# A new order for all engines, and new slots, in a fused Mamba-2 scan and SiLU feed-forward kernel

## The chip, the cores and the metric

The kernel runs on one core of one Trainium2 chip. The metric is the device time of one execution in microseconds (us). Before the change its median is 339.22 us over three runs (338.0 to 340.31).

The engines of the core are named as in the profile: PE is TensorE (matmuls), with PEld for its weight loads; DVE is VectorE, ACT is ScalarE, POOL is GpSimd, SP is SyncE, which here only issues transfers. Each engine takes its instructions in the order of the program, and waits where an operand or a buffer isn't ready; what stands behind a waiting instruction on the same engine waits with it.

## What is computed

A chunked Mamba-2 state-space scan over four batches, eight heads and 768 positions, and then a feed-forward block with SiLU on its output, reshaped to 3072 tokens of 256 features.

```python
# scan: x (4, 8, 768, 32), a (4, 8, 768), B and C (4, 8, 768, 16), chunks of 32
log_a = np.log(np.clip(a, 1e-06, 1.0))
for c in range(nc):
    cum = np.cumsum(la, axis=-1)
    L = np.exp(cum[:, :, :, None] - cum[:, :, None, :]) * causal
    M = np.einsum('bhin,bhjn->bhij', Cc, Bc) * L
    y_intra = np.einsum('bhij,bhjd->bhid', M, xc)
    y_inter = np.einsum('bhin,bhnd->bhid', Cc, state) * np.exp(cum)[:, :, :, None]
    y[:, :, sl] = y_intra + y_inter
    decay_from_j = np.exp(cum[:, :, -1:] - cum)
    Bx = np.einsum('bhjn,bhjd->bhjnd', Bc, xc) * decay_from_j[:, :, :, None, None]
    state = decay_full[:, :, None, None] * state + np.sum(Bx, axis=2)
# feed-forward: w_in (256, 2048), w_out (2048, 256)
h = x @ w_in
g = h * (1.0 / (1.0 + np.exp(-h)))
return g @ w_out
```

## The kernel before

**Units and pairs.** The scan is cut into 12 units of 256 positions (u = 0 to 11, three for a batch), each made of four chunks of 64. Two units make a pair (G or P = 0 to 5) of 512 tokens, and the feed-forward block works on pairs. Its hidden layer of 2048 is cut into eight blocks of 256 (j or i = 0 to 7).

**The order is written out.** Under a manual schedule, the string SCHEDULE lists 1283 tokens, and a loop at the end of the kernel calls one function for each. A token is a name and its arguments, so `a,1,0` calls f_a(1, 0). The sequence of the tokens is at once the sequence of the instructions of every engine and that of the transfers in each queue. Waits between engines are put in from the data: an operand that isn't written yet, or a buffer that still has readers.

**The slots.** Tiles come from four pools with numbered slots: s2k (49 of 2 KB a partition), r4k (12 of 4 KB), raw (7 of 4 KB) and hp (3 PSUM banks). SLOTS holds, for each pool, the slot of the first tile taken, of the second, and so on. A new tile in a slot waits until the last reader of the old one is done. Two more PSUM tiles, ga and gb, and a bank, o_ps, are fixed.

**The work of a unit**, with its tokens:
- loads on SP: Lx (x), Ln (B and C by position), Lt (B and C for a transpose on DVE), La (the decays, broadcast from a DRAM copy az), Lp (from a DRAM copy ac). For u = 0 and 1 the decays are made on the chip: ia, ip, A, AT, AU, as, ab, P01.
- E (DVE scan) makes the decay matrix, P (DVE scan) the prefix products, T (DVE transpose, L524) or tp with tq (PE transpose and ACT copy) the transposed B and C; ce, C and B scale C and B.
- g0 (PE, L584) makes C times B, D or gd (PE, L570) the chunk states, M (DVE) the masked matrix, b, S and SM the states from chunk to chunk, Y (PE, L634 and L643) the output.
- X0 (units 0 and 1) or y, xh and x (the others) bring the output into the feed-forward block's form. xh and x make three parts, h, l and d, of a pair's x, rounded to a format that PE multiplies in one pass.

**The feed-forward block.** Weights come as raw 512 KB blocks (lw,0 to lw,15: eight of w_in, eight of w_out). u, v (ACT), w (DVE) and W (POOL) turn each into fp32. For pair 0 the products are plain fp32: s (PE, L695), si (ACT, SiLU), n1 (PE, L759), Vn. For the pairs 1 to 5 each weight is split into three parts by H (ACT), lD and dD (DVE), and the products run in single passes: a has the h and l parts of the first matmul (eight matmuls, L798), ax rescales it in PSUM (ACT), d adds the d part (four matmuls), dg is SiLU (ACT), h (ACT), l and e (DVE, L650 and L835) split the result, q (three matmuls of 128 by 512, L780) is the second product, summed in the banks of hp and o_ps. Va, Vd, o and O scale, add, transpose and store. The last half pair goes out by Vt, ot, or and os: PE transposes, two copies, two stores.

**Warm-up.** z,1 and z,0,6 are matmuls on zeros that PE does at the start, in places where it would stand idle. ct is a SiLU on one element.

Of the kernel before, what the change touches and what calls it, by code (L numbers as in the profile page):

```python
# [28 lines left out]
si,1,3 W,4 s,0,4 si,0,4 si,1,0 Lx,2,1,0 La,2,0,0 La,2,1,0 E,2,0 W,5 s,0,5 si,0,5 W,8 n1,1,1 n1,1,0 La,3,0,0 w,11,0
w,11,1 w,9,1 s,1,4 lw,12 v,12 AD,1 Ln,2,1,0,0 tp,2 v,7 u,12 W,11 tq,2 H,1 Lt,3,1,1,0 u,10 n1,7,0 si,1,4 w,12,0 Lx,3,0,0  # L30
n1,6,1 ce,2,0 n1,0,0 E,2,1 w,7,2 lw,6 v,6 w,9,2 n1,7,1 co n1,6,0 Lp,2,0 P,2 C,2 Lt,3,1,3,0 Lx,2,0,0 B,2 gd,2 ce,2,1 g0,2
lw,13 w,14,1 La,3,1,0 W,9 b,2,0 w,10,0 S,2,0 n1,2,1 w,10,1 Lt,3,0,0,0 W,7 H,5 H,9 Lt,3,1,0,0 b,2,1 u,6 S,2,1 S,2,2
SM,2,1 SM,2,0 n1,3,1 W,10 H,10 s,0,7 si,0,7 M,2,0 n1,4,1 Lt,3,0,1,0 n1,0,1 Ln,3,0,0,0 lw,15 n1,5,0 w,6,0 H,4 w,6,2 H,2
# [10 lines left out]
Vn,1 dD,9 dD,12 h,1,2 a,1,4 Lt,5,0,0,0 Lt,5,1,0,0 n1,15,0 dg,1,1 h,1,1 Lt,5,1,3,0 T,5,1 n1,14,0 dD,3 Vn,0 lD,11 e,1,0
a,1,3 E,5,1 ax,1,4 q,1,0,1,0 q,1,0,0,0 ax,1,3 d,1,3 Ln,5,0,0,0 ce,5,0 dD,4 d,1,4 l,1,1 Lt,6,1,0,0 e,1,1 q,1,1,1,1
q,1,1,0,0 dD,6 dg,1,3 o,0,0,2 o,0,1,2 dg,1,4 Lt,5,0,2,0 q,1,0,0,1 T,5,0 ce,5,1 g0,5 Lt,6,1,3,0 E,5,0 l,1,2 B,5 h,1,3 P,5
C,5 M,5,1 q,1,0,1,1 gd,5 b,5,0 b,5,1 dD,11 q,1,1,1,0 a,1,5 e,1,2 q,1,2,0,1 h,1,4 q,1,1,0,1 H,7 ax,1,5 d,1,5 S,5,0 S,5,1
q,1,2,0,0 Lx,6,1,0 S,5,2 SM,5,0 Lt,6,1,2,0 Lt,6,1,1,0 T,6,1 ce,6,1 ce,6,0 q,1,2,1,0 Lp,6,0 Lx,6,0,0 Lt,6,0,3,0 l,1,4
# [838 lines left out]
```

## Time and profile before

| | us |
|---|---|
| median of three runs | 339.22 |
| the profiled execution's own time | 341.09 |
| its span, first to last instruction | 339.4 |
| PE busy in the span | 323.2 |
| first matmul of a token s (L695) starts | 20.31 |
| first matmul of a token a (L798) starts | 76.92 |

The prediction shows the lines of the page and of the trace. A row of a timeline gives start, length (for merged rows, from the first start to the last end), engine, line, operation, output and inputs, shapes and count; in brackets stands the time that the engine was idle just before, and what ended that. A row of a group gives busy time, mean ns of one instruction, idle time before the group's instructions and the largest releasers. "SPq" is SP's queue of transfer issues.

The page gives the granted clock of PE in 40 slices: it is full but for the second slice, at 0.7, and the last. The page's list of transfers gives 512 KB for each weight, 3.3 us from issue to landing for w_in and 7.1 for w_out as medians.

### The profile page before, as it was taken

What the parts mean: (1) busy time and instruction counts of PE and PEld (TensorE: products, weight loads), DVE (VectorE), ACT (ScalarE), POOL (GpSimd) and SP (SyncE); (2) the same over time, 40 slices, a digit from 0 to 9 for tenths busy, and PEclk for the clock granted to TensorE, in tenths of its full rate; (3) what the DMA queues carried; (4) which work ended last, traced back from release to release, by engine and by line L of the source; (5) the groups of instructions that cost most, each with busy time, mean ns of one, the idle gap of its engine ahead of it and who ended that gap; (6) DMA issues with size and microseconds to landing.
All of it is one profiled execution on the core that took longest, in us unless ns stands there. A gap on an engine that the chain in (4) does not pass through costs nothing.

```text
span 339.4 us, 7527 instructions
## 1 busy us (share of the span) xinstructions
PE 323.2 (95%) x3086; PEld 243.8 (72%) x3086; DVE 251.1 (74%) x346; ACT 201.9 (59%) x307; POOL 50.1 (15%) x64
## 2 busy tenths in 40 slices
...
GB/s 190 150 304 258 186 241 135 37 139 32 110 70 14 58 52 105 32 50 111 19 22 114 63 26 132 21 50 131 30 2 92 23 2 2 8 62 1 2 0 62
DMA packets 93522, 26.64 MB, mean 79 GB/s; under 512 B 79840, under 2 KB 86752, under 8 KB 93488
## 3 DMA queue, kind: packets, MB, share of 16 engines
...
q10 hardware_dynamic: 2352, 0.26, 0.6%
...
## 4 chain that ended last, share of the span: by engine, by line
PE 78%; DVE 8%; DMA 6%; ACT 3%; SPq 3%; issue 2%; POOL 0%; DVEq 0%
PE hp L780 28%; PE gb L798 16%; PE ga L798 16%; PE o_ps L780 5%; DMA raw<-in_moe_w_out_dram 3%; PE hp L759 2%; PE hp L695 2%; DVE ab L599 2%; PE ga L584 2%; PE ga L634 1%; DVE st L614 1%; PE ga L643 1%; DMA xt<-in_x_dram 1%; PE ga L570 1%; DVE ab L511 1%
## 5 line engine op out<-in xcount | busy, mean ns | idle before, releaser
L780 PE MATMUL hp<-r4k,s2k 128*128 128x512 f32 x400 | 110.4, 395 | 0.0
L780 PEld LDWEIGHTS hp<-r4k,s2k 128*128 128x128 f32 x400 | 73.8, 188 | 16.7 <-issue 0.7
L650 DVE SCALAR_TENSOR_TENSOR r4k<-r4k,r4k 128x1024 fp32r<-128x1024 f32 x40 | 48.8, 1221 | 32.6 <-ACT r4k L825 20.7
L798 PE MATMUL ga<-raw,s2k 128*128 128x512 f32 x240 | 63.1, 397 | 0.5 <-DVE raw L650 0.5
L798 PE MATMUL gb<-raw,s2k 128*128 128x512 f32 x240 | 62.5, 396 | 0.9 <-DVE ab L599 0.9
L798 PEld LDWEIGHTS ga<-raw,s2k 128*128 128x128 f32 x240 | 44.6, 188 | 12.3 <-DVE raw L650 1.0
L798 PEld LDWEIGHTS gb<-raw,s2k 128*128 128x128 f32 x240 | 44.3, 188 | 12.7 <-DVE ab L599 1.4
L835 DVE SCALAR_TENSOR_TENSOR r4k<-r4k,r4k 128x1024 fp32r<-128x1024 f32 x40 | 49.2, 1233 | 2.1 <-PE o_ps L780 0.2
L825 ACT ACTIVATE r4k<-r4k 128x1024 fp32r<-128x1024 f32 x40 | 42.1, 1058 | 1.1 <-DVE r4k L650 0.4
L695 PE MATMUL hp<-r4k,s2k 128*128 128x256 f32 x128 | 30.0, 384 | 1.3 <-ACT r4k L701 0.6
L809 ACT ACTIVATE ga<-ga 128x1024 f32<-128x1024 f32 x20 | 20.2, 1010 | 18.3 <-PE ga L798 18.3
L759 PE MATMUL hp<-r4k,s2k 128*128 128x512 f32 x64 | 30.7, 605 | 0.3 <-POOL s2k L318 0.3
L780 PE MATMUL o_ps<-r4k,s2k 128*128 128x512 f32 x80 | 30.7, 390 | 0.0
L809 ACT ACTIVATE gb<-gb 128x1024 f32<-128x1024 f32 x20 | 20.1, 1007 | 16.3 <-PE gb L798 16.3
L695 PEld LDWEIGHTS hp<-r4k,s2k 128*128 128x128 f32 x128 | 23.8, 190 | 8.3 <-issue 2.7
L519 POOL TENSOR_TENSOR BT<-bn,ab 128x256 f32<-128x256 f32 x10 | 9.0, 899 | 128.7 <-DVE ab L511 78.6
L318 POOL TENSOR_TENSOR s2k<-s2k,s2k 128x512 uint32<-128x512 uint32 (+1 forms) x19 | 24.4, 1298 | 21.0 <-DVE s2k L307 13.5
L819 ACT ACTIVATE r4k<-ga 128x1024 f32<-128x1024 f32 x20 | 20.5, 1025 | 9.0 <-PE ga L798 8.4
L819 ACT ACTIVATE r4k<-gb 128x1024 f32<-128x1024 f32 x20 | 20.5, 1025 | 7.8 <-PE gb L798 6.8
L511 DVE TENSOR_TENSOR_SCAN ab<-ab,diag 128x512 f32<-128x512 f32 x20 | 23.8, 1207 | 1.0 <-DMA ab<-az 1.0
L759 PEld LDWEIGHTS hp<-r4k,s2k 128*128 128x128 f32 x64 | 11.4, 189 | 9.9 <-issue 8.4
L780 PEld LDWEIGHTS o_ps<-r4k,s2k 128*128 128x128 f32 x80 | 15.0, 188 | 3.3
...
## 6 DMA issues: line engine op xcount, KB each, us to landing
...
```

What stands on the lines that cost most here:

```text
L318: nc.gpsimd.tensor_tensor(out=u[:, :, fs], in0=u[:, :, fs], in1=v[:, :, fs], op=ALU.add)
L511: nc.vector.tensor_tensor_scan(out=o, data0=src, data1=diag.rearrange("p h t -> p (h t)"), initial=0.0, op0=ALU.mult, op1=ALU.add)
L519: nc.gpsimd.tensor_tensor(out=BT[u][:, ks], in0=bn[u][:, ks], in1=E[u][:, ks, :, Q - 1:Q].to_broadcast([128, n, H, N]), op=ALU.mult)
L650: nc.vector.scalar_tensor_tensor(out=l, in0=f32(h), scalar=BACK, in1=y, op0=ALU.mult, op1=ALU.add)
L695: nc.tensor.matmul(out=hp[:, i], lhsT=WT[j][:, kc, 128 * i:128 * i + 128], rhs=XM()[:, 2 * kc:2 * kc + 2, u], start=(kc == 0), stop=(kc == ...
L759: nc.tensor.matmul(out=NP[m], lhsT=WT[8 + f // 2][:, f % 2, 128 * m:128 * m + 128], rhs=GT[0, f // 2][:, f % 2], start=(n == 1), stop=(n = ...
L780: nc.tensor.matmul(out=ACC[P, c], lhsT=WK[8 + i, p][:, k, 128 * m:128 * m + 128], rhs={"h": HT, "l": LT, "d": DT}[p][P, i][:, k], start=(n ...
L798: nc.tensor.matmul(out=o, lhsT=WK[j, q][:, kc, 128 * i:128 * i + 128], rhs=xs[:, 2 * kc:2 * kc + 2], start=(start and q == "h" and kc == 0 ...
L809: nc.scalar.activation(t, t, AF.Copy, scale=1.0 + Z)
L819: nc.scalar.activation(g, t, AF.Silu, scale=BACK)
L825: nc.scalar.activation(t, GT[G, i], AF.Copy, scale=-LESS * Z)
L835: nc.vector.scalar_tensor_tensor(out=DT[G, i], in0=f32(HT[G, i]), scalar=-1.0, in1=f32(LT[G, i]), op0=ALU.mult, op1=ALU.subtract)
```

## The change

The string SCHEDULE is replaced by another order of the same 1283 tokens, each with the same arguments and as often as before. SLOTS is replaced for all four pools, with as many entries as before. Two functions get a case for the pair 0. No operation, shape or transfer is changed.

The start of the two orders:

```diff
-ci z,1 z,1 z,1 z,0,6 z,0,6 ct z,1 z,1 cp lw,0 Ln,0,0,1,1 z,1 c1 cd z,1 ch cP ia,1 ia,0 v,0 w,0,2 cI ip,0,0 P01,0,0 u,0
...
-v,1 Ln,1,0,1,0 B,1,1 S,0,2 SM,0,1 M,0,1 ir,0 ab,1,0 E,1,0 SM,0,0 Ln,1,0,0,0 B,1,0 tp,1 ce,1,0 tq,1 ce,1,1 Y,0 w,1,0 ir,1
-ip,1,0 P01,1,0 X0,0,1 X0,0,0 S,0,3 Lx,1,1,0 w,1,1 w,1,2 W,1,0 W,1,1 P01,1,1 Lx,1,0,0 D,1 S,1,0 S,1,1 C,1 S,1,2 lw,3
-SM,1,1 w,2,0 w,2,1 W,2,0 lw,7 W,2,1 u,7 ca g0,1 M,1,1 lw,4 s,0,0 si,0,0 SM,1,0 v,3 AA,1 M,1,0 lw,9 Lx,3,1,0 u,3 AD,0 u,9
+lw,0 c1 ca ci cI z,1 z,1 co z,1 cp cd z,1 z,0,6 z,1 u,0 ia,0 ia,1 z,1 lw,2 z,0,6 ch cP v,0 A AT AU w,0,0 z,1 as,0,0
...
+C,0 z,1 Lx,0,0,0 D,0 S,0,0 as,1,0 z,1 u,2 w,2,0 lw,1 u,1 Ln,1,0,1,0 g0,0 S,0,1 M,0,1 Ln,1,1,0,0 v,1 S,0,2 SM,0,1 SM,0,0
+ab,1,0 Ln,1,0,0,0 v,2 z,0,6 W,0,0 M,0,0 Y,0 X0,0,0 X0,0,1 E,1,0 Ln,1,1,1,0 tp,1 ce,1,0 ce,1,1 w,1,0 B,1,1 S,0,3 Lx,1,0,0
+B,1,0 Lx,1,1,0 Lt,3,1,1,0 w,1,2 ip,1,0 P01,1,0 lw,3 D,1 w,1,1 tq,1 u,3 ir,0 P01,1,1 S,1,0 W,1,0 C,1 s,0,0 S,1,1 W,1,1
+H,1 S,1,2 SM,1,1 ir,3 w,2,1 w,2,2 W,2,1 g0,1 SM,1,0 M,1,0 M,1,1 lw,4 lw,11 si,0,0 s,0,1 v,3 Y,1 v,4 ir,1 u,4 w,4,2 S,1,3
+W,2,0 s,0,2 X0,1,0 w,3,2 ir,2 w,3,0 w,3,1 W,3 X0,1,1 AA,1 AD,0 lD,1 u,11 w,4,0 AA,0 AD,4 w,11,0 si,0,2 lw,5 u,5 v,5
```

The places of units 4 and 6 of which the prediction speaks:

```diff
-E,4,1 n1,13,0 H,13 Lx,4,0,0 Lt,4,1,3,0 E,4,0 Lt,4,1,0,0 T,4,1 H,8 S,3,3 y,3,0 y,3,1 xh,3 s,1,5 dD,0 Lt,4,0,2,0 x,3,0
-a,1,0 n1,9,1 si,1,5 ce,4,0 w,15,0 B,4 lD,4 lD,13 ax,1,0 n1,11,0 w,15,1 Lt,4,0,3,0 x,3,1 d,1,0 Lx,5,0,0 P,4 s,1,7 dg,1,0
-Lt,4,0,1,0 Lt,4,0,0,0 dD,2 ce,4,1 T,4,0 g0,4 w,15,2 H,14 h,1,0 lD,1 Lx,4,1,0 lD,6 lD,5 dD,5 n1,10,1 H,12 M,4,1 n1,2,0
-Lt,5,0,3,0 gd,4 Lt,5,1,2,0 M,4,0 si,1,7 b,4,0 S,4,0 n1,12,1 b,4,1 S,4,1 Ln,5,0,1,0 Lp,5,0 S,4,2 SM,4,0 lD,12 SM,4,1
+Ln,4,0,1,0 Lt,4,1,1,0 T,4,1 ce,4,0 dD,0 d,1,0 Lt,4,0,1,0 AD,2 n1,15,0 Lt,4,0,2,0 Lt,5,1,0,0 dg,1,0 Lx,5,0,0 n1,12,0
+Lt,4,0,3,0 n1,10,0 Lx,4,0,0 dD,8 P,4 C,4 H,9 ce,4,1 Ln,4,0,0,0 E,4,0 E,4,1 B,4 Lx,4,1,0 gd,4 H,2 T,4,0 g0,4 lD,5 n1,11,0
...
+Lt,6,1,2,0 d,1,7 x,5,0 h,1,5 l,1,4 dg,1,7 e,1,4 q,1,4,0,1 q,1,4,1,0 T,6,1 ce,6,1 ce,6,0 Lx,7,1,0 x,5,1 q,1,4,1,1
+Lt,6,0,0,0 E,6,1 q,1,3,1,0 Ln,6,0,0,0 Ln,6,0,1,0 B,6 Lt,6,0,2,0 Lt,7,1,3,0 T,6,0 P,6 g0,6 Lx,6,1,0 M,6,1 C,6 gd,6 M,6,0
```

ct, in the second place of ACT's order before, now stands late, among the tokens of unit 11 (`g0,11 Ln,11,0,0,0 B,11 ct gd,11`). The place of d,1,3 and the end:

```diff
+n1,14,1 n1,2,1 Ln,5,0,0,0 l,1,1 Lt,6,0,1,0 e,1,1 a,1,3 La,6,0,0 O,0,0,2,0,0 Vn,1 h,1,2 l,1,2 a,1,4 ax,1,3 d,1,3
...
-qh,5,6,1,1 q,5,4,1,1 q,5,4,0,1 qd,5,6,0,1 qd,5,7,1,1 qd,5,6,1,1 Va,5,1 Vt,5,1,1 Vt,5,1,0 O,5,0,2,2,0 ot,5,1,0 or,5,1,0
-Vt,5,1,2 Vt,5,1,3 ot,5,1,1 or,5,1,1 os,5,1,1,1 O,5,0,2,1,0 os,5,1,0,0
+qh,5,6,1,1 qd,5,6,0,1 Va,5,1 O,5,0,2,0,0 qd,5,7,1,1 qd,5,7,0,1 Vt,5,1,2 Vt,5,1,3 ot,5,1,1 Vt,5,1,0 Vt,5,1,1 ot,5,1,0
+or,5,1,0 or,5,1,1 os,5,1,1,1 os,5,1,0,0
```

The slots, here those of the PSUM banks, and the edit of the functions:

```diff
     "hp": """
-0 1 2 0 1 2 0 2 1 0 1 0 1 2 0 1 0 1 0 2 1 1 1 1 1 1 1 0 2 2 1 0 0 2 1 0 2 1 2 1 0""",
+0 1 2 0 1 2 0 2 1 0 1 2 1 2 1 2 0 1 0 2 2 1 1 1 1 1 1 2 0 1 2 0 0 1 2 0 1 2 0 1 2""",
...
-            XK[G] = [take("raw", f"XK{G}{p}", [128, 4, 2, 128], FR) for p in "hld"]
-        nc.scalar.activation(XK[G][0][:, :, v], YS[u], AF.Copy, scale=-LESS * Z)
+            XK[G] = [take("raw" if G else "r4k", f"XK{G}{p}", [128, 4, 2, 128], FR) for p in "hld"]
+        y = YS[u] if G else XM()[:, :, v]
+        nc.scalar.activation(XK[G][0][:, :, v], y, AF.Copy, scale=-LESS * Z)
...
-        y = YS[u]
+        y = YS[u] if G else XM()[:, :, v]
```

More of the change, by code (lines that the diff above doesn't have):

```diff
@@ L29 @@
[L29 to L33, printed above, removed]
@@ L44 @@
[L44 to L48, printed above, removed]
@@ new lines @@
+O,0,1,2,0,0 C,7 d,2,4 dg,2,4 SM,7,1 q,2,2,0,0 d,2,5 La,8,1,0 SM,7,0 q,2,3,1,1 dg,2,5 h,2,5 q,2,2,1,0 l,2,5 Lp,8,0
+Lt,8,0,2,0 Y,7 y,7,0 y,7,1 xh,7 x,7,0 h,2,4 O,1,1,2,2,0 S,7,3 q,2,3,1,0 La,8,0,0 E,8,0 q,2,2,0,1 e,2,5 Lx,8,1,0 a,2,7
+ax,2,7 a,2,6 Lt,8,1,0,0 q,2,5,0,0 Lt,8,1,2,0 Lt,8,1,3,0 T,8,1 ce,8,0 O,0,0,2,3,0 La,9,0,0 O,0,0,2,2,0 q,2,5,0,1 d,2,7
+Ln,8,0,0,0 ax,2,6 d,2,6 Lx,9,0,0 q,2,5,1,0 x,7,1 l,2,4 e,2,4 La,9,1,0 q,2,5,1,1 dg,2,7 ce,8,1 q,2,4,0,1 dg,2,6 q,2,2,1,1
+h,2,6 Lt,9,1,3,0 Lt,8,0,0,0 Lt,8,0,1,0 Lt,8,0,3,0 T,8,0 g0,8 h,2,7 E,8,1 Ln,8,0,1,0 B,8 gd,8 M,8,1 b,8,1 P,8 b,8,0
```

132 lines of the change are left out of this document (67 added, 65 removed), and 6 rows, old and new, of the table SLOTS.

## The prediction

> **What bounds the kernel now.** I read the page's totals first, then busy time by stretches, then what ended each idle stretch of PE.
>
> ```profile
> span 339.4 us, 7527 instructions
> PE 323.2 (95%) x3086; PEld 243.8 (72%) x3086; DVE 251.1 (74%) x346; ACT 201.9 (59%) x307; POOL 50.1 (15%) x64
> PE 78%; DVE 8%; DMA 6%; ACT 3%; SPq 3%; issue 2%; POOL 0%; DVEq 0%
> ```
>
> PE is busy 95% of the span and is 78% of the chain that ended last. All PE work is kept, so the time is PE's 323.2 us plus its idle time, 339.4 - 323.2 = 16.2 us. Where that idle time lies is in the busy times by stretches (columns: stretch, length, then busy time of PE, PEld, DVE, ACT, POOL, the granted clock, DMA share, GB/s); I cut at the first stage-one matmul (20.31) and the first matmul of the second method (76.92):
>
> ```profile
> 0.00:20.31 20.31, 14.50 (x286) 9.29 (x286) 15.85 (x38) 10.39 (x21) 6.87 (x19) 0.92 0.82 192
> 20.31:76.92 56.61, 52.33 (x573) 35.02 (x565) 45.52 (x72) 36.27 (x74) 28.42 (x31) 1.00 0.69 177
> 76.92:320.00 243.08, 241.34 (x2172) 187.69 (x2171) 180.08 (x226) 148.45 (x204) 14.78 (x17) 1.00 0.26 50
> 320.00:339.38 19.38, 15.05 (x67) 11.85 (x65) 9.64 (x13) 6.78 (x8) 0.00 (x0) 0.94 0.12 27
> ```
>
> Idle PE: 20.31 - 14.50 = 5.8 us at the start, 56.61 - 52.33 = 4.3 in the middle, 243.08 - 241.34 = 1.7 in the long third stretch, 19.38 - 15.05 = 4.3 at the end. So a new order can win little: the third stretch is full, and the start and the end are latency. It can lose more easily, by leaving PE uncovered in a stretch that is full today. What PE waited for in the middle (timeline of PE alone; in brackets its idle time and what ended it):
>
> ```profile
> 24.49 0.27 PE L634 MATMUL ga<-cw,sm 32*64 32x64 f32 x2 [0.46 <-ACT sm L622]
> 34.20 7.55 PE L695 MATMUL hp<-r4k,s2k 128*128 128x256 f32 x32 [0.64 <-ACT r4k L701]
> 46.02 0.44 PE L530 MATMUL o_ps<-ident,tbc 128*128 128x128 f32 x2 [0.60 <-DMA tbc<-in_C_dram]
> 52.52 0.33 PE L584 MATMUL ga<-ce,bh 32*64 32x128 f32 x2 [1.06 <-ACT ce L545]
> 78.28 1.66 PE L798 MATMUL ga<-raw,s2k 128*128 128x512 f32 x6 [0.54 <-DVE raw L650]
> ```
>
> **The change part by part.** Both texts hold the same 1283 tokens, so nothing is added or removed; the edit to f_XH and f_XL acts on G = 0 alone, and the first such token of either text is xh,2, of G = 1. It costs nothing.
>
> *The start.* In the old order PE has tp,1 (L530) ahead of Y,0 (L634), in the new one Y,0 comes first.
>
> ```profile
> 15.63 0.64 ACT L622 ACTIVATE sm<-st,par 128x96 f32<-128x96 f32 x2 [0.87 <-DVE st L614]
> 16.96 0.66 PE L530 MATMUL o_ps<-ident,s2k 128*128 128x128 f32 x4 [2.03 <-DMA s2k<-in_B_dram]
> 20.31 0.48 PE L695 MATMUL hp<-r4k,s2k 128*128 128x256 f32 x1
> ```
>
> Y,0's last operand, sm, was there at 15.63 + 0.64 = 16.27, but PE stood 2.03 us for the B load of unit 1 that tp,1 needs, and began Y,0 after 16.96 + 0.6. So Y,0 can start 1.3 us sooner. The four loads that tp,1 wants go from places 15 to 19 of SP's queue to 13 to 16, so tp,1 isn't late behind it. Not all of it arrives: the next PE steps, s,0,1 and Y,1, want W,1 and M,1, and the DVE operations up to M,1 are nearly the same set in both orders. I take **-1.0 us** (0 to -1.6).
>
> *The table load.* The token ct, a Silu on one element, was ACT's first; it now stands near the end, and the first function ACT meets is Abs (u,0).
>
> ```profile
> 0.80 1.28 ACT L388 ACT_TABLE_LOAD   x1 [0.80 <-PEq L870]
> 23.57 0.58 ACT L701 ACTIVATE r4k<-hp 128x512 f32<-128x512 f32 x1
> 24.34 0.66 ACT L297 ACTIVATE s2k<-raw 128x512 f32<-128x512 uint32 x1
> 24.89 0.68 ACT L294 ACTIVATE s2k<-raw 128x512 f32<-128x512 f32 x1
> 27.68 0.38 ACT L665 ACTIVATE r4k<-ga 128x256 f32<-128x256 f32 x1
> 28.11 5.45 PE L695 MATMUL hp<-r4k,s2k 128*128 128x256 f32 x24 [0.21 <-ACT r4k L665]
> ```
>
> One load of 1.28 us, at 0.80, served Silu, Abs and Copy. If the load for Abs brings tables without Silu, a second load stands in front of si,0,0, behind SM,1,0. From there ACT has, up to X0,1,1: si,0,0, v,3, v,4, u,4 and two X0, 0.58 + 2 x 0.66 + 0.68 + 2 x 0.38 = 3.3 us; PE covers it with Y,1 and s,0,2, which took 28.11 - 0.21 - 24.49 = 3.4 us. The cover is 0.1 us, so most of a second load would be seen at s,1,1. No row tells whether it comes: between 0 and +1.3 us, I take **+1.0**. The Trainium skill speaks against the change here (ScalarE: Activation LUTs, sections "What ACT_TABLE_LOAD costs" and "Table sets: the hidden batching unit"): tables come in sets with one costly function each, Abs and Copy being filler in all of them, and it measured about 1283 ns for a load, which the row confirms, plus about 1380 ns of drain. By it a second load is likely, and with its 2.66 us the sum below would be some 1.4 us higher.
>
> *The middle.* Of the 4.3 us idle there, the five waits above are 3.3. The order that made them is gone: s,0,3 has another place and another bank, and C of unit 2 is asked for three n1 ahead of tp,2 instead of just ahead. What stays is ce,2,0 just ahead of g0,2 and x,3,0 just ahead of a,1,0. DVE, 45.5 of 56.6 us busy here and 49.9 of 53.1 in the first part of the next stretch (first row below), gets less to do before the same PE work: ahead of a,2,0 the old text has eight DVE tokens that the new one puts behind it, one l, one e, one E and five shorter, and the new one has one l that the old one hasn't.
>
> ```profile
> 76.92:130.00 53.08, 52.29 (x552) 36.66 (x551) 49.88 (x73) 31.87 (x50) 6.39 (x7) 1.00 0.27 57
> ...
> L650 DVE SCALAR_TENSOR_TENSOR r4k<-r4k,r4k 128x1024 fp32r<-128x1024 f32 x40 | 48.8, 1221 | 32.6 <-ACT r4k L825 20.7
> L835 DVE SCALAR_TENSOR_TENSOR r4k<-r4k,r4k 128x1024 fp32r<-128x1024 f32 x40 | 49.2, 1233 | 2.1 <-PE o_ps L780 0.2
> L511 DVE TENSOR_TENSOR_SCAN ab<-ab,diag 128x512 f32<-128x512 f32 x20 | 23.8, 1207 | 1.0 <-DMA ab<-az 1.0
> ```
>
> That is at least 1221 + 1233 + 1207 - 1221 = 2.4 us less DVE work ahead, for two q (1.4 us of PE) less ahead. I take half of the idle time as won, **-2.0** (from -4.3, all of it, to +1.2, if two more waits like the median one, 0.6, come than go).
>
> *The loads of the later units.* SP issues in order and waits with each load for its buffer, so a load that follows one of a blocked buffer is late. It was blocked much in the old order too:
>
> ```profile
> SPq L262 <- DVE ct L524: 34.3, 6, 13.9
> L269 SPq DMA_DIRECT2D xt<-in_x_dram x20: 376/446/813, 18.5 to 233.4; - x20
> DMA to landing us min/median/max: 3.0/3.6/4.2
> 75.99 0.61 DVE L524 STREAM_TRANSPOSE ct<-tbc 128x256 f32<-128x256 f32 x1
> 76.56 0.43 SPq L269 DMA_DIRECT2D xt<-in_x_dram  x1
> 86.78 0.45 PE L570 MATMUL ga<-xt,BT 64*32 64x64 f32 x32
> 166.49 1.81 PE hp L780 x8
> 101.84 1.72 PE hp L759 x4
> ```
>
> The second and third rows are L269's own answer: 0.45 us for an issue, 3.0 to 4.2 us to landing. The old order hid that: Lx,4,1 was issued at 76.56, soon after the transpose T,4,1 (75.99), and gd,4, which reads it, came at 86.78, 10.2 us later. In the new text two loads of x have lost that lead. For gd,6: Lt,7,1,3 overwrites what T,6,1 reads, so SP stands until that transpose is done, and Lx,6,1 is next behind it. It lands 0.45 + 3.6 = 4.05 us after T,6,1, and between T,6,1 and gd,6 PE has two q and g0,6, six matmuls of 1.81 / 8 = 0.227 and about 0.45, 1.8 us: 2.25 us uncovered. For gd,4: Lt,5,1,0 waits for T,4,1, and four more issues stand between it and Lx,4,1, so it lands 5 x 0.45 + 3.6 = 5.85 us after T,4,1; PE has d,1,0 and three n1, 4 x 0.227 + 3 x 0.86 = 3.5 us: 2.35 us uncovered. The loads of units 8 and 11 are close as well, with some 6 us of PE work behind T,8,1 and T,11,1. If DVE reaches its transposes ahead of PE's place in the text, part is hidden: 0 to 4.6 for the two, **+3.0** taken. The other loads I looked at keep leads above the landing time.
>
> *Thin covers in the full stretch.* At d,1,3 the new order leaves between a,1,3 and d,1,3 only a,1,4, 1.81 us, while ACT has Vn,1, h,1,2 and ax,1,3:
>
> ```profile
> L768 ACT ACTIVATE r4k<-hp 128x512 f32<-128x512 f32 x2 | 1.2, 598 | 1.7 <-PE hp L759 1.7
> L825 ACT ACTIVATE r4k<-r4k 128x1024 fp32r<-128x1024 f32 x40 | 42.1, 1058 | 1.1 <-DVE r4k L650 0.4
> L809 ACT ACTIVATE gb<-gb 128x1024 f32<-128x1024 f32 x20 | 20.1, 1007 | 16.3 <-PE gb L798 16.3
> ```
>
> 0.60 + 1.06 + 1.01 = 2.67, so 0 to 0.9 us as the first two start before or after a,1,3 ends. a,1,5 close behind M,5,1 and q,2,5,0,0 close behind e,2,5 are alike. For all of them **+0.8** (0 to 2.7, three times 0.9). Other slots of the pools make no wait of their own that I find: each tile's slot is last read well ahead of its new writer, those of s,0,1 and s,0,2 excepted, which lie in the start's and the table load's terms.
>
> *The end.*
>
> ```profile
> 333.45 0.60 ACT L785 ACTIVATE r4k<-hp 128x512 f32<-128x512 f32 x1 [1.44 <-PE hp L780]
> 334.43 0.89 DVE L725 SCALAR_TENSOR_TENSOR r4k<-o_ps,r4k 128x128 f32<-128x128 f32 x4 [0.95 <-PE o_ps L780]
> 335.74 0.42 DVE L745 COPY s2k<-gb 128x256 f32<-128x256 f32 x1 [0.42 <-PE gb L737]
> ```
>
> Behind the last h or l matmul come Va,5,1 (0.60) and three d matmuls (0.68) instead of four, then the same four Vt, two transposes, two copies and stores, the halves swapped: **0** (±0.3).
>
> **Sum.** -1.0 + 1.0 - 2.0 + 3.0 + 0.8 = +1.8 us. The profiled execution took 341.09 us around its span of 339.4; the median of the three is 339.22, and the sum is put on that: 341.0 us, +0.5%. About 1%, 3.4 us, is what a measurement can tell from no change, so "within 1%" is 335.8 to 342.6.
>
> **The rivals.** First, slower: the late loads cost in full. SP's order lets x of units 4 and 6, then B or the transposed tiles of 8 and 11, land behind their place, 2.3 us each, 9 instead of 3.0: 341.0 + 6.2 = 347 us. It decides from the point at which DVE runs its transposes at their place or later; from 4.6 of the 9 us on, the time is past 342.6. For it: DVE was busy 50 of 53 us behind 76.92, so it can't be far ahead, and T,4,1 at 75.99 stood close to the matmuls it is next to in the text. Against it: less DVE work lies ahead of the same PE work now.
>
> Second, faster: the loads are hidden by a DVE that has got ahead, no second table load comes, and the middle's waits go: -1.0 - 4.3 + 0 + 0 + 0.8 = -4.5, 334.7 us. For it: the five waits each had one cause that the order has moved. Against it: the two loads of x have no lead by the text, and DVE, which has to get ahead for them to be hidden, stays as busy as now.
>
> Third, nothing to see because the changes of place are hidden: with each term at its small end the time is 339, inside the forecast's class.
>
> **Numbers.** Within 1%, the forecast and the third together, 0.44; the late loads or a like loss past 342.6, 0.35; the faster case, 0.21. The forecast's own range is 336 to 342.6. For 8 in 10 it must reach into both others: down to 335, short of the whole faster case, up to 347, the whole price of the late loads.
>
> **What would show it.** Right: Y,0 ahead of the four L530 and the first L695 near 19; a second ACT_TABLE_LOAD ahead of the first L701; less than 4.3 us of PE idle from the first L695 to the first L798; PE rows with "<-DMA xt" at the L570 of units 4 and 6. Wrong: no such rows and a third stretch as full as 1.7 us idle, which would leave only gains; or idle PE there ended by ACT or DVE in many small pieces, which the covers I looked at don't hold.

## The result, and the profile after

| | before | after |
|---|---|---|
| median of the executions | 338.57 us (8, 337.84 to 340.31) | 335.22 us (8, 333.64 to 336.57) |
| ratio, 95% interval | | 0.9892 (0.9863 to 0.9922) |
| profiled execution, its span | 341.09, 339.4 | 334.10, 332.4 |

The changed kernel is about 1.1% faster, 3.35 us. The two profiled executions differ by more, 7.0 us, since the one of before lies 2.5 us above its median and the one of after 1.1 us below. A reading of these two traces alone doubles the effect, so other executions stand beside them below. One execution of the run with later x loads and two of the last weight-chain run were in a slower state of the chip, and are left out of their medians and ratios.

The page of the changed kernel: totals, then the shares of the chain that ended last.

```profile
span 332.4 us, 7531 instructions
PE 321.6 (97%) x3085; PEld 243.9 (73%) x3086; DVE 248.9 (75%) x346; ACT 203.2 (61%) x308; POOL 49.1 (15%) x64
PE 85%; SPq 5%; DMA 3%; issue 3%; DVE 2%; POOL 1%; ACT 0%; POOLq 0%; DVEq 0%
```

Its busy times by stretches, cut where those of before were cut: at the first s step, at a,1,0 and 19.4 us ahead of the end (columns as above: stretch, length, busy time of PE, PEld, DVE, ACT, POOL, granted clock, DMA share, GB/s).

```profile
0.00:18.41 18.41, 14.54 (x253) 8.67 (x254) 13.18 (x33) 9.24 (x18) 5.89 (x20) 1.00 0.76 165
18.41:71.56 53.15, 50.99 (x605) 35.28 (x595) 47.27 (x77) 38.41 (x79) 27.93 (x26) 1.00 0.73 198
71.56:313.00 241.44, 240.88 (x2174) 187.92 (x2173) 179.79 (x226) 149.28 (x206) 15.31 (x18) 1.00 0.27 52
313.00:332.40 19.40, 15.23 (x68) 12.07 (x66) 8.61 (x12) 6.26 (x8) 0.00 (x0) 0.98 0.13 27
```

Length less PE's busy time is its idle time: 3.87, 2.16, 0.56 and 4.17 us, where before had 5.81, 4.28, 1.74 and 4.33. That is 5.4 us less, and PE's own work took 1.6 less. Ahead of a,1,0 stand 858 matmuls in the changed kernel (253 + 605) and 859 in the other (286 + 573), and the changed kernel is there 5.4 us sooner. What is left of waits, and the places that the prediction named, in the timelines of PE, ACT, DVE and SP of the changed kernel (start, length; in brackets the idle time and what ended it; the new code is one line longer, so s is L696, si L702, a and d L799):

```profile
16.15 0.27 PE L634 MATMUL ga<-cw,sm 32*64 32x64 f32 x2 [1.02 <-ACT sm L622]
17.44 0.66 PE L530 MATMUL o_ps<-ident,s2k 128*128 128x128 f32 x4
18.41 1.99 PE L696 MATMUL hp<-r4k,s2k 128*128 128x256 f32 x8
21.64 1.97 PE L696 MATMUL hp<-r4k,s2k 128*128 128x256 f32 x8 [0.61 <-DVE st L614]
...
22.05 0.68 ACT L622 ACTIVATE sm<-st,par 128x128 f32<-128x128 f32 x2
22.75 1.28 ACT L702 ACT_TABLE_LOAD   x1
24.04 0.60 ACT L702 ACTIVATE r4k<-hp 128x512 f32<-128x512 f32 x1
...
29.87 1.35 PE L696 MATMUL hp<-r4k,s2k 128*128 128x256 f32 x5 [1.06 <-POOL s2k L318]
...
73.44 0.64 DVE L524 STREAM_TRANSPOSE ct<-tbc 128x256 f32<-128x256 f32 x1
76.20 1.28 PE L799 MATMUL ga<-raw,s2k 128*128 128x512 f32 x4
76.67 0.93 SPq L269 DMA_DIRECT2D xt<-in_x_dram  x1
80.07 0.46 PE L570 MATMUL ga<-xt,BT 64*32 64x64 f32 x32
...
118.75 0.69 DVE L524 STREAM_TRANSPOSE ct<-tbc 128x256 f32<-128x256 f32 x1
119.83 0.43 SPq L269 DMA_DIRECT2D xt<-in_x_dram  x1
122.97 0.46 PE L570 MATMUL ga<-xt,BT 64*32 64x64 f32 x32
...
256.66 0.43 PE L570 MATMUL ga<-xt,BT 64*32 64x64 f32 x24 [0.56 <-POOL BT L519]
```

Y,0 stands ahead of tp,1 and the first s step is at 18.41; the second table load came, at 22.75; and the two L570 rows at 80.07 and 122.97, gd,4 and gd,6, have no bracket. PE didn't wait for the late x loads at all. Waits are left at Y,0 (for SM), s,0,1 (for S,1,2), s,1,3 (for W,3) and gd,11 (for B,11).

### The profile page after: what moved, and what is told of

It is laid out like the page before. It is cut to its first block, busy times and chain, and to the rows that moved or that the text cites. A ratio compares the mean times of both kernels' runs of the same rounds, so it can differ in the third digit from the quotient of the medians.

```text
span 332.4 us, 7531 instructions
## 1 busy us (share of the span) xinstructions
PE 321.6 (97%) x3085; PEld 243.9 (73%) x3086; DVE 248.9 (75%) x346; ACT 203.2 (61%) x308; POOL 49.1 (15%) x64
## 4 chain that ended last, share of the span: by engine, by line
PE 85%; SPq 5%; DMA 3%; issue 3%; DVE 2%; POOL 1%; ACT 0%; POOLq 0%; DVEq 0%
PE hp L781 27%; PE ga L799 16%; PE gb L799 15%; PE hp L760 9%; PE hp L696 6%; PE o_ps L781 5%; PE ga L634 1%; PE ga L643 1%; PE ga L584 1%; SPq L254 1%; DMA raw<-in_moe_w_in_dram 1%; PE ga L570 1%; SPq L262 1%; DMA bn<-in_B_dram 1%; PE gb L643 1%
## 5 line engine op out<-in xcount | busy, mean ns | idle before, releaser
L799 PE MATMUL gb<-raw,s2k 128*128 128x512 f32 x240 | 62.8, 397 | 0.0
L799 PE MATMUL ga<-raw,s2k 128*128 128x512 f32 x240 | 62.0, 394 | 0.0
L799 PEld LDWEIGHTS gb<-raw,s2k 128*128 128x128 f32 x240 | 44.2, 188 | 12.1 <-ACT gb L810 1.4
L799 PEld LDWEIGHTS ga<-raw,s2k 128*128 128x128 f32 x240 | 44.4, 188 | 11.0 <-ACT ga L810 1.2
L696 PE MATMUL hp<-r4k,s2k 128*128 128x256 f32 x128 | 29.8, 383 | 1.7 <-POOL s2k L318 1.1
L696 PEld LDWEIGHTS hp<-r4k,s2k 128*128 128x128 f32 x128 | 23.7, 190 | 8.0 <-POOL s2k L318 2.6
L519 POOL TENSOR_TENSOR BT<-bn,ab 128x256 f32<-128x256 f32 x10 | 7.6, 757 | 121.2 <-DVE ab L511 98.3
```

The lines of the kernel that those rows point to most:

```text
L519: nc.gpsimd.tensor_tensor(out=BT[u][:, ks], in0=bn[u][:, ks], in1=E[u][:, ks, :, Q - 1:Q].to_broadcast([128, n, H, N]), op=ALU.mult)
L696: nc.tensor.matmul(out=hp[:, i], lhsT=WT[j][:, kc, 128 * i:128 * i + 128], rhs=XM()[:, 2 * kc:2 * kc + 2, u], start=(kc == 0), stop=(kc == ...
L799: nc.tensor.matmul(out=o, lhsT=WK[j, q][:, kc, 128 * i:128 * i + 128], rhs=xs[:, 2 * kc:2 * kc + 2], start=(start and q == "h" and kc == 0 ...
```

## The experiments

All ratios are to the kernel before, with 95% intervals. That kernel was measured anew with each group of runs (medians 338.57 to 339.39 us), so a small difference between runs of different groups is better read from the ratios than from the medians. "Idle" is PE's idle time in the run's profile in three stretches (to the first s step; from there to a,1,0; from there to the end), length less busy time as above; the two kernels themselves have 5.8, 4.3, 6.1 and 3.9, 2.2, 4.7 us. Where two orders are joined, the first is followed as far as told, and then every step not yet done comes in the second's order. All runs that take parts of both orders, and the old order with ct last, have their slots given out anew; the other edits keep the slots of the kernel they start from. The idle sums in some of the expectations are of another kind and count only the single waits that the profile lists, some 12.4 us for the kernel before and 7.1 for the changed one.

**The second execution of the changed kernel** (no edit).

> The changed kernel once more, for a second look at its waits. If its waits belong to the order: again none at gd,4 and gd,6, about 1.06 us at s,1,3, 0.5 to 2 us at gd,11, PE idle in sum 7 to 8.5 us, ratio to the kernel before 0.986 to 0.992. If the first look was a lucky execution: waits at gd,4 or gd,6 in this one, or a ratio above 0.992.

335.24 us, ratio 0.9877 (0.9851 to 0.9904); idle 4.5, 2.5, 6.1. No wait at gd,4 or gd,6; s,1,3 stood 1.05 us, gd,11 2.04. The idle sum is 13.1, where the first execution has 10.8. The listed waits alone make 9.5, above the 8.5 that I expected at most, but the places are the same. The waits at s,1,3 and the lack of any at the x loads belong to the order; the size of those at Y,0, s,0,1 and gd,11 changes from execution to execution.

**One half of the change at a time**, joined at a,1,0.

```diff
-old order up to a,1,0
+changed order up to a,1,0
 old order for the rest
```

> The changed order up to the first a step, the old order for everything behind it. Theory H (the gain is made ahead of the first a step, where PE's idle time fell from 10.09 to 6.03 us between the two profiles, and the rest is neutral): 3 to 4 us under the kernel before, ratio 0.988 to 0.991, PE idle ahead of the first L798 about 6 us, the second table load still there. Theory R (the gain is made behind it, where PE's idle fell from 6.07 to 4.73): within 1 us of the kernel before, ratio 0.997 to 1.002.

```diff
 old order up to a,1,0
-old order for the rest
+changed order for the rest
```

> The old order up to the first a step, the changed order for everything behind it. Theory H: within 1 us of the kernel before, ratio 0.997 to 1.002. Theory R: 3 us or more under it, ratio 0.991 or less. Theory L (the late loads of my prediction are real, and the changed head, which brings the PE to the first a step with less old VectorE work queued, is what covers them): waits for the x load at gd of units 4 and 6, up to 2.35 and 2.25 us, and 2 to 4 us over the kernel before.

Neither gained: 340.36 us, 1.0013 (0.9987 to 1.0039), and 339.46 us, 1.0009 (0.9977 to 1.0042). Idle 3.3, 1.9, 8.8 in the first: its head is as good as the changed kernel's, and the joint loses it again. One row of PE's timeline there:

```profile
79.41 1.17 PE L798 MATMUL ga<-raw,s2k 128*128 128x512 f32 x4 [2.69 <-DVE raw L653]
```

This is d,1,0. The changed head leaves a different set of VectorE steps for later, and the old order puts two E scans, a T and others in front of x,3,1, on which d,1,0 waits. In the second, idle is 4.7, 4.6, 5.7, and there is no wait at gd,4 or gd,6 either: theory L fell, since the late loads are hidden behind the old head too. H foresaw the second run rightly and the first one not, R the first and not the second.

**Joined at unit 6**, where the sets of steps done differ least.

```diff
-old order up to gd,6
+changed order up to gd,6
 old order for the rest
```

> The changed order up to gd of unit 6, where the two orders have nearly the same set of steps behind them, and the old order for the rest; the first seam, at a,1,0, cost a wait of 2.7 us at d,1,0. Theory H (the gain is made in the first part, and the first hybrid lost it at its seam): PE idle in sum 7 to 8.5 us for 12.5, and 3 to 5 us under the kernel before, ratio 0.985 to 0.991. Theory R (it takes the changed order of the whole to gain): within 1 us of the kernel before.

338.06 us, 0.9978 (0.9952 to 1.0004); idle 4.6, 3.3, 7.1. Again a wait at the joint, 1.81 us at a,1,6, and the old order's own 0.94 at a,3,5. Less than H foresaw, so H isn't shown by this run; the time fits R, within 1 us of the kernel before.

**Y of unit 0 first, in the old order.**

```diff
-tp,1 ce,1,0 tq,1 ce,1,1 Y,0 w,1,0 ir,1 ip,1,0 P01,1,0 X0,0,1 X0,0,0
+Y,0 X0,0,1 X0,0,0 tp,1 ce,1,0 tq,1 ce,1,1 w,1,0 ir,1 ip,1,0 P01,1,0
```

> The old order with one move: Y and X0 of unit 0 put ahead of the four transposes of unit 1 (tp,1). Theory S (what the changed head gains at the start is this move): first L695 1 to 2 us earlier (18.3 to 19.3 for 20.31) and 1 to 1.9 us under the kernel before, ratio 0.9945 to 0.997. Theory W (the next PE steps, s,0,1 and Y,1, want W,1 and M,1, which the move doesn't hasten): first L695 earlier, but the time within 0.5 us of the kernel before.

339.27 us, 0.9989 (0.9962 to 1.0017); first s at 20.59, idle 6.1, 3.7, 5.9. Nothing gained, and not even the first s came earlier.

**The changed start on the old rest**, twice: plainly, and with the loads that unit 1 wants put right behind the start.

```diff
-old order up to Y,0 and its X0
+ci ct
+changed order up to Y,0 and its X0
 old order for the rest
```

> The changed order up to the first Y and its two X0, with the one-element Silu at the start, and the old order for the rest. Theory S (the new order of the set-up work on VectorE, which brings AT 1.5 us earlier, 5.53 for 7.03, is worth its time): PE idle ahead of the first s step 3.3 to 4.0 us for 4.7 to 5.8 with the old order, 1 to 2 us under the kernel before, ratio 0.994 to 0.997. Theory W (the weights and VectorE's queue behind it take it back): within 0.5 us of the kernel before, with more idle time between the first s and a,1,0 than the 4.3 us of the kernel before.

```diff
 X0,0,1
-ir,2 ir,3
+Ln,1,1,1,0 Lx,1,0,0 Lx,1,1,0 ip,1,0 ir,2 ir,3
```

> The changed start on the old rest once more, with the seam mended: the four loads of unit 1 that D,1 and P01,1 want stand directly behind the start, ahead of ir,2 and ir,3 (in the first trial D,1 stood 4.28 us for x). Theory S (the changed start is worth its time): no wait over 0.5 us at D,1, PE idle ahead of the first s 3.3 to 4.5 us for 4.7 to 6.1, 1 to 2 us under the kernel before, ratio 0.994 to 0.997. Theory W (what is gained ahead of the first s is waited for behind it): within 0.5 us, and 1 us or more of added idle time between the first s and a,1,0.

340.81 us, 1.0071 (1.0048 to 1.0094), and 340.13 us, 1.0039 (1.0017 to 1.0061). The first stood 4.28 us at D,1 for x; the second mended that (1.01 us at D,1, now for B,1 from POOL) and still lost; idle 5.2, 4.6, 5.6. What the changed start does is plain in the two traces. Two rows of VectorE's timeline in the kernel before, and AT's row on PE:

```profile
4.82 0.69 DVE L310 SCALAR_TENSOR_TENSOR s2k<-raw,s2k 128x512 uint32<-128x512 uint32 x1 [1.46 <-ACT s2k L297]
...
6.61 0.21 DVE L445 TENSOR_SCALAR s2k<-s2k 32x128 f32<-32x128 f32 x1
7.03 0.22 PE L450 MATMUL o_ps<-ident,s2k 32*128 32x32 f32 x1 [1.25 <-issue]
```

The same steps in the changed kernel's timelines:

```profile
5.10 0.21 DVE L445 TENSOR_SCALAR s2k<-s2k 32x128 f32<-32x128 f32 x1 [1.83 <-DMA s2k<-in_a_dram]
5.53 0.28 PE L450 MATMUL o_ps<-ident,s2k 32*128 32x32 f32 x1 [0.43 <-DVE s2k L446]
6.63 0.69 DVE L310 SCALAR_TENSOR_TENSOR s2k<-raw,s2k 128x512 uint32<-128x512 uint32 x1
```

In the old order A stands behind w,0,2, which waits for a weight; in the changed one A goes as soon as its own load has landed, and AT is 1.5 us earlier. On the old rest nothing of that was left.

**The two waits of unit 2, mended in the old order.** ACT's row in the kernel before shows why g0,2 stood there: ce,2,1 waited for VectorE's C,2, which reads the same tile.

```profile
51.99 0.47 ACT L545 ACTIVATE ce<-o_ps,par 128x256 f32<-128x256 f32 x1 [1.57 <-DVE cw L550]
```

```diff
-Ln,2,0,0,0 ... Ln,2,1,0,0 tp,2 ... ce,2,0 ... C,2 ... gd,2 ce,2,1 g0,2
+Ln,2,0,0,0 Ln,2,1,0,0 ... tp,2 ... ce,2,0 ce,2,1 ... C,2 ... gd,2 g0,2
```

> The kernel before with two moves in unit 2: the C load Ln,2,1,0 put behind Ln,2,0,0 (tp,2 waits 0.5 to 1.3 us for it in the four looks at the old order), and ce,2,1 directly behind ce,2,0, ahead of C,2 (in the old order ACT stood 1.57 us at ce,2,1 until DVE had read the same tile in C,2, and g0,2 1.0 to 1.3 us for ce,2,1). Theory H (the middle's part of the gain is single waits that the order made, 1.6 us): both waits gone, PE idle between the first s and a,1,0 2.2 to 3.0 us for 3.7 to 4.6, 1.0 to 2.2 us under the kernel before, ratio 0.9935 to 0.997. Theory V (VectorE's total work, not single waits, holds this part back, and another wait takes their place): within 0.5 us, ratio 0.9985 to 1.0015.

339.5 us, 1.0010 (0.9988 to 1.0031); idle 5.2, 4.0, 5.9. Both waits went, and two others took their place on PE (n1,7,0 and n1,2,1, for weights that POOL's W makes):

```profile
44.97 4.56 PE L759 MATMUL hp<-r4k,s2k 128*128 128x512 f32 x10 [0.91 <-POOL s2k L318]
...
51.34 1.98 PE L759 MATMUL hp<-r4k,s2k 128*128 128x512 f32 x4 [0.83 <-POOL s2k L318]
```

**Start and middle together** (both edits above).

> Both: the changed start and the two moves in unit 2, the rest in the old order. Theory H (start and middle are the gain, and they add): 2.2 to 3.8 us under the kernel before, ratio 0.989 to 0.9935, PE idle in sum 8 to 9.5 us for 11.5 to 12.5. Theory V/W (they are waited for later): under 1 us.

343.0 us, 1.0131 (1.0111 to 1.0150). Idle is 5.0, 3.4, 5.9 in the profiled execution, which took 339.52; the other four took 342.78 to 344.06, and no profile shows what they lost. That stays open; no part of it is a gain.

**The weight chain.** The steps lw, u, v, w, W, s, si and n1 take the other order's sequence, in the places that such steps have; the few H, lD, Vn and o that would stand ahead of what they read are moved behind it. What pointed there is VectorE's wait at L303 (w,n,0) for ACT's u. The waits of VectorE in the kernel before, from 20 to 62 us (columns: total, times, longest):

```profile
DVE s2k L303 <- ACT s2k L294: 9.7, 4, 3.3
```

The same in the changed kernel, from 18 to 57 us:

```profile
DVE s2k L303 <- ACT s2k L294: 0.2, 1, 0.2
```

```diff
-lw 3 7 4 9 14 5 8 11 10 12 6 13 15 ... s,0,2 s,1,2 s,1,1 s,1,0 s,0,3 s,1,3 ...
+lw 3 4 11 5 7 10 8 6 12 9 14 13 15 ... s,0,2 s,1,1 s,1,3 s,1,0 s,0,3 s,1,2 ...
```

> The old order, but the steps of the feed-forward weights and of the first method (lw, u, v, w, W, s, si, n1) stand in the changed kernel's sequence, in the places that such steps have in the old order (one H and one Vn moved behind the step that they read). Theory K (what the changed order wins in the middle is the sequence of the weight chain: in the old one VectorE stood 9.7 us between 20 and 62 us at L303 for ACT's u, and ACT 6.7 us for weight loads, in the changed one 0.2 at L303 and 1.2 for loads): VectorE's wait at L303 below 5 us, PE idle between the first s and a,1,0 1.5 to 3.0 us for 3.7 to 4.6, and 1.5 to 3.5 us under the kernel before, ratio 0.990 to 0.9955. Theory J (it takes the places of all steps to fit together): within 1 us of the kernel before or above it.

and the reverse in the changed order:

> The reverse: the changed order with those steps in the old sequence (six H, lD, Vn and o moved behind what they read). Theory K: VectorE's wait at L303 above 5 us, PE idle between the first s and a,1,0 3.5 us or more for 1.9 to 3.3, 1.5 to 4 us over the changed kernel, ratio 0.992 to 1.001. Theory J: also above the changed kernel, by waits in many places, though L303 need not stand. If the sequence is of no account: ratio 0.986 to 0.990.

356.06 us, 1.0504 (1.0471 to 1.0536), and 349.8 us, 1.0301 (1.0252 to 1.0350). The first is 17 us slower than the kernel before, the second some 14.5 us slower than the changed one. In the first, VectorE's wait at L303 fell to 1.9 us as K wanted, and others came (8.6 us at L310, w,n,2, for ACT's v; PE 4.7 us at Y,3); in the second that wait was back at 6.0 us, also as K wanted, but PE stood 5.5 us at two s steps for W, and the loss is several times what K foresaw. K's cause isn't the cause by itself; J fits better: sequence and places fit each other or lose.

**The late x loads, one transpose later**, in the changed kernel.

```diff
-Lx,4,1,0 gd,4 H,2 T,4,0
+T,4,0 Lt,5,0,0,0 Lx,4,1,0 gd,4 H,2
...
-Lx,6,1,0
+Lt,7,0,0,0 Lx,6,1,0
```

> The changed kernel with the second x loads of units 4 and 6 put one transpose later on SP's queue: T,4,0 and a tbc load of the next unit (which waits for that transpose) stand ahead of Lx,4,1, and such a load ahead of Lx,6,1. In the changed kernel's trace T,4,0 ended at 79.64 and gd,4 began at 80.07, T,6,0 ended at 121.65 and gd,6 began at 122.97; an x load landed 2.8 us after its issue. Theory L (the mechanism of my late-loads term is real and the changed kernel missed it by less than a microsecond): waits of 2.5 to 3.3 us at gd,4 and 1.5 to 2.3 us at gd,6, and 4 to 5.6 us over the changed kernel, so about as long as the kernel before, ratio 1.000 to 1.006. Theory M (the loads are hidden anyway, whatever their place): as the changed kernel, ratio 0.988 to 0.991.

342.77 us, 1.0118 (1.0065 to 1.0170), some 7.5 us over the changed kernel. The waits are the ones expected, at gd,4 and gd,6 (PE's timeline of this run):

```profile
83.72 0.35 PE L570 MATMUL ga<-xt,BT 64*32 64x64 f32 x16 [2.56 <-DMA xt<-in_x_dram]
...
130.84 0.35 PE L570 MATMUL ga<-xt,BT 64*32 64x64 f32 x16 [2.22 <-DMA xt<-in_x_dram]
```

and the loss is larger than their sum, 4.8 us. The stretch from a,1,0 to the end and two pieces of it, by windows:

```profile
72.30:342.30 270.00, 260.25 (x2240) 202.11 (x2238) 188.97 (x237) 155.57 (x213) 15.27 (x18) 0.98 0.25 49
84.70:88.10 3.40, 3.40 (x4) 1.41 (x5) 2.96 (x7) 2.04 (x5) 0.00 (x0) 0.50 0.86 151
132.50:135.90 3.40, 3.40 (x10) 2.63 (x9) 3.25 (x8) 1.45 (x3) 0.00 (x0) 0.50 0.42 129
```

About 1 and 1.7 us behind each wait PE ran 3.4 us at half the clock, and its busy time in this stretch is 260.25 us for some 256.1 in the changed kernel. So theory L holds, with a second price on top that it hadn't.

**The table load.** In the changed kernel, ct first; in the old one, ct last; and once more in a mended version (below).

```diff
-lw,0 c1 ca ci cI ... B,11 ct gd,11
+lw,0 c1 ca ci ct cI ... B,11 gd,11
```

> The changed kernel with the one-element Silu put back to the start, so that no second table load stands ahead of the first si step. Theory T (the load costs what my prediction took, 1.0 us, 0 to 1.3): 0.5 to 1.3 us under the changed kernel, which is 3.9 to 4.7 under the kernel before, ratio 0.986 to 0.9885, and the wait at s,1,3 (1.06 us for W,3) shorter. Theory N (the load is hidden beside PE's Y,1 and s,0,2): as the changed kernel, ratio 0.989 to 0.991.

```diff
-ci ... ct ... gd,11
+ci ... ct gd,11
```

> The kernel before with its one-element Silu moved to unit 11. Theory T: a second table load of 1.28 us ahead of the first si step, a wait of 0.5 to 1.3 us at the s steps behind it, 0.3 to 1.3 us over the kernel before, ratio 1.001 to 1.004. Theory N (PE's Y,1 and s,0,2 cover it in the old order): the load is there, but the time is within 0.3 us, ratio 0.999 to 1.001.

334.35 us, 0.9839 (0.9794 to 0.9885), 0.9 us under the changed kernel, which the scatter of the executions could hide, and the wait at s,1,3 is 0.2 for 1.06; in the old order 339.37 us, 1.0006 (0.9986 to 1.0026): the load was there, Y,1 stood 1.21 us for 0.46, and nothing of it was left at the end.

**Mending the changed order.** Its own waits, by the rows above, six moves and then a seventh:

```diff
-lw,0 c1 ca ci cI ... ct gd,11
+lw,0 c1 ca ci ct cI ... gd,11
-S,0,0 as,1,0 z,1 u,2 w,2,0 lw,1 u,1 ... S,0,1 M,0,1 ... v,1 S,0,2 SM,0,1 SM,0,0
+S,0,0 S,0,1 S,0,2 as,1,0 z,1 u,2 w,2,0 lw,1 SM,0,1 SM,0,0 u,1 ... M,0,1 ... v,1
-Lx,1,1,0 Lt,3,1,1,0 w,1,2 ip,1,0
+Lx,1,1,0 ip,1,0 Lt,3,1,1,0 w,1,2
-C,1 s,0,0 S,1,1 W,1,1 H,1 S,1,2
+s,0,0 S,1,1 W,1,1 H,1 S,1,2 C,1
-Ln,11,0,1,0 ... g0,11 Ln,11,0,0,0 B,11
+Ln,11,0,1,0 Ln,11,0,0,0 ... g0,11 B,11
```

> The changed kernel with six moves: the one-element Silu first; the load ip,1,0 ahead of Lt,3,1,1; S,0,1 and S,0,2 right behind S,0,0 and both SM of unit 0 ahead of u,1 (Y,0 stood 1.0 us for SM); C,1 behind S,1,2 (s,0,1 stood 0.4 to 0.6 for S,1,2); Ln,11,0,0 beside Ln,11,0,1 (gd,11 stood 0.6 and 2.0 us for B,11). Theory P (each wait goes and nothing takes its place): Y,0 at about 15.1, 1.4 to 3.4 us under the table-load run, 331 to 333 us, ratio 0.976 to 0.981. Theory Q (what is gained at Y,0 is waited for at the next s steps, and only gd,11 gains): 0.5 to 1.5 us under it, ratio 0.980 to 0.984.

332.35 us, 0.9811 (0.9776 to 0.9846): by the medians 2.0 under the table-load run, by the ratios 0.9, and the intervals overlap. The waits at s,0,1, s,1,3 and gd,11 are gone; Y,0 still stood, 1.56 us, now for M,0,0, which has w,2,0 ahead of it on VectorE, as in the changed kernel. The seventh move puts w,2,0 behind it:

```diff
-S,0,2 as,1,0 z,1 u,2 w,2,0 ... M,0,1 ... M,0,0 Y,0
+S,0,2 as,1,0 z,1 u,2 ... M,0,1 ... M,0,0 w,2,0 Y,0
```

> The mended kernel with one move more: w,2,0 behind M,0,0, since there Y,0 stood 1.56 us for M,0,0, which had w,2,0 ahead of it on VectorE, and a half-clock window from 16.6 to 20.0 us followed that wait. Theory P (the wait goes, and the window with it): Y,0 at 14.5 to 15.2, first s step at 17.3 to 18.0 for 19.15, 1 to 2.5 us under the mended kernel, 329.9 to 331.4 us, ratio 0.974 to 0.978. Theory Q (the next s steps wait for W and si instead): within 0.6 us of the mended kernel, ratio 0.979 to 0.983.

and the same kernel with ct back at unit 11:

> The run before this with the one-element Silu back at unit 11, as the change has it, so that a second table load stands ahead of the first si step again. Theory T (the load costs about its 1.28 us, seen in the changed kernel and three hybrids as a wait of 1.05 to 1.07 us for W,3 at s,1,3, which was 0 with the Silu first): a wait of 0.8 to 1.3 us at s,1,3 and 0.8 to 1.3 us over the run before this. Theory N (that wait was another's): no such wait, within 0.4 us.

332.08 us, 0.9794 (0.9771 to 0.9817): the fastest here, 2.1% under the kernel before and some 3 us under the changed one, though little under the run before it (Q's side): Y,0 stood 0.72 us for 1.56, but began at 15.89 for 15.94. Its idle by stretches is 18.24 - 14.89 = 3.4, then 0.7, then 4.2, nearly all of it start and end:

```profile
0.00:18.24 18.24, 14.89 (x255) 8.69 (x255) 13.26 (x33) 9.50 (x19) 5.67 (x20) 1.00 0.83 182
18.24:70.15 51.91, 51.19 (x604) 35.39 (x595) 48.18 (x78) 37.28 (x78) 27.91 (x26) 1.00 0.72 197
70.15:330.40 260.25, 256.09 (x2240) 199.96 (x2238) 188.15 (x237) 155.43 (x212) 15.32 (x18) 1.00 0.25 50
```

With ct late it took 334.11 us, 0.9836 (0.9809 to 0.9862): 2.0 us more (1.4 by the ratios), and in its timelines the load and the wait are back:

```profile
23.62 1.28 ACT L702 ACT_TABLE_LOAD   x1
24.92 0.60 ACT L702 ACTIVATE r4k<-hp 128x512 f32<-128x512 f32 x1
...
30.73 1.56 PE L696 MATMUL hp<-r4k,s2k 128*128 128x256 f32 x6 [1.07 <-POOL s2k L318]
```

## Why the prediction was wrong

It gave 341.0 us, +1.8; the time fell by 3.35. The step that failed is the term **late loads, +3.0**. It measured 0, in both executions of the changed kernel and behind the old head too. The need was sized a little long: for gd,4 I had 5.85 us from T,4,1's end to the landing of x. The rows give 76.67 - (73.44 + 0.64) = 2.6 us to the issue, and this load landed 2.8 us behind its issue, so 5.4. The line's own answer, here that of the changed kernel, knows the landing of two transfers only, 2.8 for this load and 3.8 for one of the start:

```profile
DMA to landing us min/median/max: 2.8/3.3/3.8
```

The 3.6 that I took from the same row of the kernel before is likewise the middle of two, 3.0 and 4.2, both issued ahead of 20 us. The larger error was the lead. I counted the PE work that the text puts between T,4,1 and gd,4, 3.5 us, as if VectorE reached T,4,1 when PE reached that place. It was there 2.1 us sooner (end 74.08, d,1,0 begins at 76.20), and from T,4,1's end to gd,4's start there are 6.0 us. For gd,6 it is 122.97 - 119.44 = 3.5 us for the 1.8 that I counted; PE didn't stand there, so x, issued at 119.83, landed in at most some 3.3 us. The case named as "part is hidden" was the whole of it, and what I held against it, a VectorE 50 of 53 us busy, says how full its queue is and not how far ahead of PE it runs. The mechanism is real: one transpose later, both waits came at their price. The changed kernel is less than a microsecond from them, 0.6 us at gd,4.

*Thin covers, +0.8:* 0. No wait at d,1,3, a,1,5 or q,2,5,0,0; the third stretch's idle time is 0.56 and 2.04 us in the two executions, all of it one wait at gd,11, for the B load of unit 11. I had called the loads of unit 11 close, and priced them only in the slower rival; they cost just these waits, which the mended kernel doesn't have.

*The table load, +1.0:* it came, at the place foretold, and costs 2.0 us by the medians of one pair of runs (1.4 by their ratios) and 0.9 by another that isn't clear of the scatter. Its way to PE was another: not X0 and s,1,1, which didn't wait, but the v steps behind it, then w and W,3, to s,1,3. Six traces of the changed head with the load have that wait at 1.05 to 1.07 us, and three of them 0.36 to 0.52 us more at the s step behind Y,1, for the Silu itself. The sum for 1283 ns plus a drain of about 1380 ns (the Trainium skill, ScalarE: Activation LUTs, "What ACT_TABLE_LOAD costs") isn't borne out: the load begins 0.02 us behind SM and the Silu 0.01 us behind the load, so ACT lost 1.28 us and no drain is to be seen. That tables come in sets is borne out: with Silu met first one load served Silu, Abs and Copy, and with Abs met first a second load came at the first Silu.

*The start, -1.0:* the size was near, the reason wrong, so the size was luck. PE's idle time there is 5.8, 4.7, 5.0 and 5.2 us in four traces with the old start, and 3.9, 4.5, 3.3, 3.5 and 4.6 in five with the changed one: means of 5.2 and 3.9, -1.2. The 2.03 us that tp,1 stood for B was one execution's: three other traces with the same order there have no such wait, and Y,0 begins at 16.2 to 16.3 us in them, where the five with the changed start have 14.8 to 16.2. Y,0 moved by itself gained nothing. What the rows show of the change at the start is A and AT brought forward.

I also passed over the granted clock, 0.92 in the first stretch of the kernel before. In five traces with the old start the clock stands at 0.50 for some 3.4 us, from 8 to 9 us on, and in ten of twelve with the changed start, mended or not, at 1.00 throughout that stretch; the other two have the half clock later, behind a wait at D,1 or at Y,0. By what is on record it doesn't explain the gain: the second trial of the changed start on the old rest has 1.00 too and lost, and of 101 executions of the kernel before, with mean clocks from 0.984 to 1.000, the 26 at 0.999 or more took 339.5 us on average and the 27 at 0.992 or less 339.2.

*The middle, -2.0:* it measured -2.1 between the two profiles, with the table load's wait inside. By more traces it is less: 2.2, 2.5, 1.9, 3.1 and 3.3 us idle with the changed order, 4.3, 4.6, 4.0 and 3.7 with the old one (the last with Y,0 moved), so -1.6; without that load's 1.06 it would be some 2.6, more than I took. The fifth of the waits that I listed, 0.54 us at 78.28, lies behind a,1,0 and not in this stretch, so the waits listed were 2.8 of its 4.3 us. That the waits had one cause each is refuted for those of unit 2: mended, they came back at other steps.

*The end, 0:* 4.33 to 4.17 us.

Without the two terms that were nothing, the sum would have been -2.0, and 337.2 us; from the same 339.22 the time fell by 4.0, so some 2 us of the gain are in no term. **Of the rivals,** the faster one (334.7) lies next to the result; it was right that the loads are hidden by a VectorE that has got ahead, and wrong that no table load comes and that all of the middle's 4.3 us go, so that it came so close is in part luck.

**What is shown, and what isn't.** Shown: late loads and thin covers cost nothing in the changed order, gd,11 apart; the table load and the waits that are left cost it 3 us (335.24 us against 332.08 in the same group of runs), 1.4 to 2.0 of them by the load. The gain itself is fewer PE waits ahead of a,1,0: five traces with the changed head have 5.2 to 7.9 us of idle time there, four with the old one (Y,0 moved in one) 9.0 to 10.1. From a,1,0 to the end the two executions of the changed kernel took 260.8 and 262.7 us and the kernel before 262.5, so no gain is clear there. Which moves bring the gain wasn't found: every part put into the other order (two heads, two starts, Y,0, unit 2, the weight chain) gained nothing that can be measured or lost. That it takes the order as a whole is what all of these agree with, not a proof. A rival was left untested: no run has the changed order with other slots, and the mixed orders had new slots as well as new places, so a part of their loss may be the slots'. Against that stands one run, the old order with ct last, whose slots differ in three of the four pools and which took 1.0006 of the time before.
